# Every engine's instructions in one written order of 1785 steps, parameter loads on three queues, and two row tiles in one FFT step

## The chip, the cores and the metric

The kernel runs on one core of one Trainium2 chip. The metric is the device time in microseconds (us) of one execution. The kernel before takes 423.82 us (the median of 3 runs, 423.2 to 435.42). A core has five engines, each with its own stream of instructions that it works through in order: PE (TensorE, matrix products into the eight PSUM banks), DVE (VectorE, elementwise), ACT (ScalarE, functions, and here all copies out of PSUM), POOL (GpSimd) and SP (SyncE). Here POOL and SP mostly issue DMAs. Semaphores make an instruction wait for what it needs from another engine or from a DMA.

## What is computed

Two independent parts with 2048 positions and 640 channels each, put side by side in the output. Cut to what matters:

```python
# A: attention over a dilated window of 8 positions (32 heads of 20)
qkv = (x @ wqkv).reshape(B, S, 3, H, Dh)             # q, k, v per head
idx = pos[:, None] - 2 * jnp.arange(8)[None, :]      # i, i-2, ..., i-14
logits = einsum("bhsd,bhswd->bhsw", q, k[idx]) * Dh ** -0.5   # -1e9 where idx < 0
o = einsum("bhsw,bhswd->bhsd", softmax(logits), v[idx])
a = o.reshape(B, S, D) @ wo

# B: a state-space convolution (192 states per channel)
logdA = dt * (A_re + 1j * A_im)
K = einsum("dn,dnl,dn->dl", C, exp(logdA[:, :, None] * l), dt * (B_re + 1j * B_im)).real   # 2048 taps
y = irfft(rfft(u padded) * rfft(K padded))[:2048] + u * Dskip
```

## The kernel before

**Part A.** Projections (`proj`, L427, letters k, q, v of the order): 15 groups of four matmul chains of 512 columns; ACT copies each out (L428), SP stores it to DRAM (`qd`, `kd`, `vd`). Attention goes by blocks b of 512 positions. `logits` (L): DVE multiplies q with shifted k (tile `prod`, L464), PE sums within heads (L466, `ps_l`), ACT takes the exponential. `norm` (N) divides by the sum. `av` (A, 20 of them): four loads of `vb` from `vd` on SP and POOL (two `vb` buffers), two DVE products `p` (L504, two `p2` buffers), eight matmuls into `ps_o` (L506), a copy to `oT`. `out_proj` (O, 16): ten matmuls (L517, `ps_op`), two copies to `ob` (two buffers), one store on SP (L520).

**Part B.** `partB_prep` loads the six parameter tensors (`nat`, L123), transposes and scales them on PE (`flip`, L142 and L146) and makes `ta` (ACT), `wi` and `Gt` (DVE). The 640 channels then go in five chunks c of 128. `gens` (G) makes the powers of the recurrence: Exp and Sin on ACT, products on DVE, stored to DRAM (`Gdram`) for all chunks but the first. `x_tables` (T loads `Xg`, M computes) and `y_tables` (D decay factors on ACT, W loads, Y computes) build factor tables by complex products on DVE (L226 to L228, L289). `kgen` (K) contracts them on PE: 512 small matmuls a chunk (L303, `ps_k`, one PSUM bank) in three rounds, each copied out by ACT (L305). The kernel K goes through DRAM (l, `kload`) and is spread to 2048 taps (g, `ps_s`). A two-step FFT of u (f) and of K (g): `f1` (L343) and `f2_prod` (x, L363), the product with DVE (L368, `Yf`). Then the inverse: `ia` (y, L378, the matmuls `ps_ia` with the constant `EA`, copied out by ACT to `Z`, L380) and `inverse` (I, L737, `ps_ib`), which needs the 4 MB constant `HB`. `skip` (S) computes u * Dskip from `uq`. `HB` lies in the memory of the tables, which is free when the last K stage has ended. U stages bring u into another layout.

**What sets the order.** `ORDER` lists 144 stages, each a call that emits all its instructions. From these the framework's scheduler makes the order on every engine when the program is built, by readiness and by place in the list; whatever it decides is then fixed, and each engine works through its own list. Part of a stage may so come before another's. PSUM is shared as two banks "a" (`ps_p`, `ps_op`), three "b" (FFT steps), two "l" (attention, transposes), and one for `ps_k`.

Of the kernel before, what the change touches and what calls it, by code (L numbers as in the profile page):

```python
# [17 lines left out]
NCH = 5  # L18
CW = 192
ORDER = "k3 q4 q2 D0 U4 q0 U1 q1 q3 k4 G0 G1 M0 v4 Y0 k1 U7 U0 k0 k2 K0 U5 v0 v1 v2 U6 L0 U3 T1 L1 v3 N0 A0 A1 U2 A2 A3 A4 G3 L2 D1 L3 W1 R0 O2 N1 M1 Y1 T2 O3 O0 l0 f0 M2 K1 D2 O1 g0 x0 W2 T3 Y2 A5 A6 K2 A7 f1 l1 g1 y0 W3 x1 D3 M3 T4 Y3 A8 A9 L4 y1 K3 L5 W4 N2 l2 M4 D4 O6 O5 f2 O4 g2 x2 l3 Y4 O7 A10 y2 K4 S1 S0 f3 A11 g3 A12 A13 A14 O9 O11 x3 y3 O8 L6 O10 S3 L7 f4 l4 N3 A15 S2 g4 A16 A17 A18 x4 A19 I1 I2 y4 S5 I0 S4 S6 I3 I4 S7 O14 O12 I5 O13 I7 I6 O15"  # L20
# [15 lines left out]
XGB = 1  # L36
# [39 lines left out]
def fft_consts_np():  # L76
# [11 lines left out]
    EA = np.zeros((128, 4, 64, 2, 2))  # L88
    for dd in range(2):
        s = slice(64 * dd, 64 * dd + 64)  # L90
        EA[s, 0, :, 0, dd] = np.cos(phi)
        EA[s, 0, :, 1, dd] = np.sin(phi)
        EA[s, 1, :, 0, dd] = -np.sin(phi)
        EA[s, 1, :, 1, dd] = np.cos(phi)
# [8 lines left out]
    return dict(BD1=BD1.reshape(128, 256), T=T.reshape(128, 32 * 2 * 64), EA=EA.reshape(128, 1024), HB=HB.reshape(128, 64 * 2 * 128))  # L103


def partB_prep(tc, pools, prm, Gd):

    nc = tc.nc
    V = nc.vector
    pp, psp, ident, ap = pools["prep"], pools["psum"], pools["ident"], pools["att"]  # L110
    W = NCH * CW
    nat = []
    for tag in ("p2", "p2", "prod"):
        nt = ap.tile([128, 2, NCH, CW], bf16, name="nat", tag=tag, bufs=2)
        nat += [nt[:, 0], nt[:, 1]]
    ldt = pp.tile([128, NCH], bf16, name="ldt")
    lsrc = prm["B_log_dt"].rearrange("(g c t) -> g t c", g=4, c=NCH, t=32)
    for g in range(4):
        nc.scalar.dma_start(out=ldt[32 * g:32 * g + 32, :], in_=lsrc[g])
    for a, nm in enumerate(["B_A_re", "B_A_im", "B_C_re", "B_C_im", "B_B_re", "B_B_im"]):  # L120
        src = prm[nm].rearrange("(g c t) n -> g t c n", g=4, c=NCH, t=32)
        for g in range(4):
            (nc.gpsimd if a in (2, 3) else nc.sync).dma_start(out=nat[a][32 * g:32 * g + 32], in_=src[g])  # L123
    qt = pp.tile([128, 1], f32, name="quarter")
    nc.gpsimd.memset(qt[:], float(np.pi / 2))
    pools["quarter"] = qt
    dtb = pp.tile([128, NCH], bf16, name="dtb")
    nc.scalar.activation(out=dtb[:], in_=ldt[:], func=ACT.Exp)
    dtf = pp.tile([128, NCH], f32, name="dtf")
    V.tensor_copy(out=dtf[:], in_=dtb[:])  # L130
    dg = ap.tile([128, NCH, 128], bf16, name="dg", tag="attn")
    for c in range(NCH):
        V.tensor_scalar(out=dg[:, c, :], in0=ident[:], scalar1=dtf[:, c:c + 1], scalar2=None, op0=A.mult)

    def flip(a, diag, tag="l"):
        psb = [psp.tile([128, 512], f32, name="ps_tr", tag=tag, bufs=2 if tag == "l" else 3) for _ in range(2)]
        for c in range(NCH):
            rhs = dg[:, c, :] if diag else ident[:]
            for h in range(2):
                hs = slice(64 * h, 64 * h + 64)  # L140
                col = c * CW + 64 * h
                nc.tensor.matmul(psb[col // 512][:, col % 512:col % 512 + 64], lhsT=nat[a][:, c, 0:128], rhs=rhs[:, hs], start=True, stop=True, skip_group_check=True)  # L142
            for h in range(2):
                hs = slice(64 * h, 64 * h + 64)
                col = c * CW + 128
                nc.tensor.matmul(psb[col // 512][hs, col % 512:col % 512 + 64], lhsT=nat[a][hs, c, 128:192], rhs=rhs[hs, hs], start=True, stop=True,  # L146
                                 tile_position=(64 * h, 64 * h), skip_group_check=True)
        return [(slice(0, 512), psb[0][:]), (slice(512, W), psb[1][:, 0:W - 512])]

    ta = pools["cst"].tile([128, W], f32, name="ta")  # L150
    wi = pp.tile([128, W], i32, name="wi")
    for s, ps in flip(0, True):
        nc.scalar.copy(out=ta[:, s], in_=ps)
    wk = ap.tile([128, 512], f32, name="wk", tag="qb")
    for s, ps in flip(1, True):
        n = ps.shape[1]
        V.tensor_scalar(out=wk[:, 0:n], in0=ps, scalar1=1.0 / TWO_PI, scalar2=MAGIC, op0=A.mult, op1=A.add)
        V.tensor_scalar(out=wk[:, 0:n], in0=wk[:, 0:n], scalar1=MAGIC, scalar2=None, op0=A.subtract)
        V.scalar_tensor_tensor(out=wk[:, 0:n], in0=ps, scalar=1.0 / TWO_PI, in1=wk[:, 0:n], op0=A.mult, op1=A.subtract)
        V.tensor_scalar(out=wi[:, s], in0=wk[:, 0:n], scalar1=2147483648.0, scalar2=None, op0=A.mult)  # L160
    cc = ap.tile([128, 2, W], bf16, name="cc", tag="prod", bufs=2)
    for i in range(2):
        for s, ps in flip(2 + i, False):
            nc.scalar.copy(out=cc[:, i, s], in_=ps)
    Gt = ap.tile([128, NCH, 2, CW], bf16, name="Gt", tag="oT")
    br, bi = flip(4, True, "b"), flip(5, True)
    pr = [ap.tile([128, W], f32, name="pr", tag=t, bufs=n) for t, n in (("kb", 1), ("vb", 2))]
    for op, c0, c1, r in ((A.subtract, 0, 1, 0), (A.subtract, 1, 0, 1)):
        for (s, b0), (_, b1) in zip(br, bi):
            V.tensor_tensor(out=pr[0][:, s], in0=b0, in1=cc[:, c0, s], op=A.mult)  # L170
            if r == 0:
                V.tensor_tensor(out=pr[1][:, s], in0=b1, in1=cc[:, c1, s], op=A.mult)
            else:
                V.scalar_tensor_tensor(out=pr[1][:, s], in0=b1, scalar=-1.0, in1=cc[:, c1, s], op0=A.mult, op1=A.mult)
        p3 = [pr[q][:].rearrange("p (c n) -> p c n", c=NCH) for q in range(2)]
        if r == 0:
            V.tensor_tensor(out=Gt[:, :, 0], in0=p3[0], in1=p3[1], op=A.subtract)
        else:
            V.tensor_tensor(out=Gt[:, :, 1], in0=p3[1], in1=p3[0], op=A.subtract)
    nc.sync.dma_start(out=Gd[1:, :, NG - 1].rearrange("c p r n -> p c (r n)"), in_=Gt[:, 1:].rearrange("p c r n -> p c (r n)"))  # L180
    return ta, wi, Gt


def gens(tc, pools, ta, wi, ca, cb, dst, done):

    nc = tc.nc
    V = nc.vector
    gp = pools["prep"]
    n = cb - ca
    s = slice(CW * ca, CW * cb)  # L190
    order = [3, 4, 5, 6, 7, 8, 0, 1, 2, 9, 10]
    am = gp.tile([128, 11, 2 * CW], bf16, name="am", tag="am")
    for k in order:
        nc.scalar.activation(out=am[:, k, 0:n * CW], in_=ta[:, s], func=ACT.Exp, scale=float(2 ** k))
    for k in order:
        pht = gp.tile([128, 2 * CW], i32, name="ph", tag="ph", bufs=2)
        mct = gp.tile([128, 2 * CW], f32, name="mc", tag="mc", bufs=2)
        ph, mc = pht[:, 0:n * CW], mct[:, 0:n * CW]
        if dst is None:
            cst = gp.tile([128, 2, 2, CW], bf16, name="cs", tag="cs", bufs=2)  # L200
            cs = cst[:, 0:n]
        else:
            cs = dst(k)
        V.tensor_scalar(out=ph, in0=wi[:, s], scalar1=k + 1, scalar2=None, op0=A.logical_shift_left)
        nc.scalar.activation(out=mc, in_=ph, func=ACT.Abs, scale=PHS)
        v = lambda ap: ap.rearrange("p (c n) -> p c n", c=n)
        nc.scalar.activation(out=cs[:, :, 1], in_=v(ph), func=ACT.Sin, scale=PHS)
        nc.scalar.activation(out=cs[:, :, 0], in_=v(mc), func=ACT.Sin, scale=-1.0, bias=pools["quarter"][:])
        V.tensor_tensor(out=cs, in0=cs, in1=v(am[:, k, 0:n * CW]).unsqueeze(2).to_broadcast([128, n, 2, CW]), op=A.mult)
        done(k, cs)  # L210


def decay(tc, pools, ta, c):


    S = pools["tab"].tile([128, MID, CW], bf16, name="Stab", tag="Stab")
    for k in range(1, MID + 1):
        tc.nc.scalar.activation(out=S[:, k - 1], in_=ta[:, CW * c:CW * c + CW], func=ACT.Exp, scale=float(-16 * k))  # L218
    pools["S", c] = S


def cmul(nc, O, Y, g, t, conj):

    V = nc.vector
    for o, gr in ((O[0], g[0]), (t[0], g[1])):
        V.tensor_tensor(out=o, in0=Y, in1=gr, op=A.mult)  # L226
# [41 lines left out]
def y_tables(tc, pools, Y, c):  # L268
# [12 lines left out]
    for k in range(1, 4):  # L281
        ys(2 ** k + 1, 2 ** k - 1, 2 ** k)
# [527 lines left out]
```

The softmax here doesn't subtract the row's maximum and nothing guards it: scores larger than these inputs give would overflow.

## Time and profile before

| | busy, us | instructions |
|---|---|---|
| PE matmul | 329.0 (78% of 422.1) | 6100 |
| PE weight loads | 211.1 | 6100 |
| DVE | 315.4 (75%) | 472 |
| ACT | 290.4 (69%) | 612 |
| POOL | 85.6 (20%) | 158 |
| DMA | 72.65 MB, mean 172 GB/s | |

The costliest groups are L427 (`ps_p`, 77.1 us for 300 matmuls), L303 (`ps_k`, 51.7 us for 2560), L504 and L464 on DVE (47.8 us each), the copies L346 and L365 on ACT (42.5 and 41.1 us) and L378 (`ps_ia`, 39.5 us for 320 matmuls). An engine's busy time is the union of its records, which can overlap; a line's total can hence count a little more. A wait is put down to what ended it last. "Issue" is time in which an engine waits for nothing that the profile shows. The mean granted clock of PE was 0.903 of full speed.

### The profile page before, as it was taken

The page shows a single profiled execution, that of the slowest core. Times are in us where ns is not written, and L with a number is a line of the kernel's source. Part 1 is how long each engine was busy: PE and PEld are TensorE (multiplying, and loading weights), DVE is VectorE, ACT ScalarE, POOL GpSimd, SP SyncE. Part 2 cuts the span into 40 slices and gives each one's busy share as a digit, 9 for nine tenths or more (in the row PEclk, how much of TensorE's full clock was granted, in tenths as well). Part 3 has the DMA queues.
Part 4 walks back from the last instruction along what each step waited for, and adds up shares of the span by engine and source line. Part 5 has one row for each costly group of instructions (what it writes and reads, how often), then busy time and mean ns, then how long its engine had stood idle before and what let it go on. Part 6 is the DMA issues. An engine that isn't in the chain of part 4 may idle for free.

```text
span 422.1 us, 14233 instructions
## 1 busy us (share of the span) xinstructions
PE 329.0 (78%) x6100; PEld 211.1 (50%) x6100; DVE 315.4 (75%) x472; ACT 290.4 (69%) x612; POOL 85.6 (20%) x158
## 2 busy tenths in 40 slices
PE   0476896989698144897989889958798898978982
PEld 0342342455432013655668657746486756655871
DVE  1339996733998999689999989958997057778472
ACT  1586895999897976267997377734866285789731
POOL 6313350150001233402111201001111022012242
PEclk9999698999999755599999899966998899999996
DMA  7994865686655858627733263242432099646977
GB/s 179 243 213 104 240 178 204 240 247 216 207 136 217 264 155 247 174 75 208 215 107 101 80 202 124 78 129 85 128 114 90 5 313 320 187 167 180 221 145 149
DMA packets 67996, 72.65 MB, mean 172 GB/s; under 512 B 32421, under 2 KB 58261, under 8 KB 67165
## 3 DMA queue, kind: packets, MB, share of 16 engines
q1 hardware_dynamic: 60076, 55.28, 44.8%
q0 software_dynamic: 6496, 15.64, 13.8%
q10 hardware_dynamic: 1360, 0.82, 0.9%
q8 instruction: 48, 0.79, 0.8%
q14 instruction: 16, 0.12, 0.1%
HBM read 44.11 MB, written 24.98 MB: 164 GB/s over the span
## 4 chain that ended last, share of the span: by engine, by line
PE 43%; ACT 21%; DMA 15%; DVE 11%; issue 7%; SPq 1%; DVEq 0%; ACTq 0%
PE ps_k L303 8%; PE ps_ia L378 7%; PE ps_f L343 6%; PE ps_p L427 5%; DMA out_dram<-ob 4%; ACT S L365 4%; PE ps_op L517 4%; PE ps_o L506 3%; ACT A L346 2%; DMA Gdram<-cs 2%; PE ps_l L466 2%; ACT Stab L218 2%; DMA nat<-in_B_A_im_dram 2%; PE ps_f L363 2%; PE ps_ib L737 2%
## 5 line engine op out<-in xcount | busy, mean ns | idle before, releaser
L427 PE MATMUL ps_p<-xT,w 128*128 128x512 bf16 x300 | 77.1, 410 | 13.8 <-ACT st L428 13.3
L303 PE MATMUL ps_k<-Ytab,Xtab 128*20 128x33 bf16 (+1 forms) x2560 | 51.7, 246 | 13.5 <-issue 11.5
L504 DVE TENSOR_TENSOR p<-vb,attn 128x2048 bf16<-128x2048 bf16 x40 | 47.8, 1218 | 17.7 <-PE ps_o L506 16.4
L427 PEld LDWEIGHTS <-w 128*128 128x128 bf16 x300 | 30.1, 103 | 56.5 <-issue 29.8
L303 PEld LDWEIGHTS <-Xtab 128*20 128x20 bf16 (+1 forms) x2560 | 45.0, 126 | 24.0 <-issue 20.6
L464 DVE TENSOR_TENSOR prod<-qb,kb 128x2048 bf16<-128x2048 bf16 x40 | 47.8, 1220 | 7.6 <-PE ps_l L466 5.6
L346 ACT CAST A<-ps_f 128x512 bf16<-128x512 f32 x80 | 42.5, 608 | 10.1 <-PE ps_f L343 10.0
L500 POOL DMA_DIRECT2D vb<-vd x40 | 22.6, 569 | 124.3 <-DVE p L504 118.6
L378 PE MATMUL ps_ia<-cEA,Yf 128*128 128x256 bf16 x320 | 39.5, 279 | 5.5 <-DVE Yf L368 3.5
L365 ACT CAST S<-ps_f 128x512 bf16<-128x512 f32 x80 | 41.1, 621 | 1.6 <-PE ps_f L363 1.3
L517 PE MATMUL ps_op<-wo,oT 128*128 128x320 bf16 x160 | 32.9, 320 | 7.3 <-ACT oT L508 3.6
L428 ACT CAST st<-ps_p 128x512 bf16<-128x512 f32 x60 | 34.0, 581 | 5.3 <-PE ps_p L427 5.3
L380 ACT CAST Z<-ps_ia 128x512 bf16<-128x512 f32 x40 | 23.5, 593 | 20.2 <-PE ps_ia L378 19.5
L378 PEld LDWEIGHTS <-Yf 128*128 128x128 bf16 x320 | 30.7, 100 | 12.9 <-DVE Yf L368 4.7
L363 PE MATMUL ps_f<-A,cT 128*64 128x128 bf16 x640 | 31.5, 222 | 2.7 <-ACT A L346 0.8
L368 DVE TENSOR_TENSOR Yf<-S 128x1024 bf16<-128x1024 bf16 x40 | 25.6, 686 | 6.5 <-ACT S L365 6.5
L506 PE MATMUL ps_o<-p,cG 128*32 128x512 bf16 x160 | 22.2, 437 | 10.6 <-DVE p L504 10.5
L363 PEld LDWEIGHTS <-cT 128*64 128x64 bf16 x640 | 21.8, 109 | 15.5 <-issue 13.8
L305 ACT CAST Kd<-ps_k 128x363 bf16<-128x363 f32 (+1 forms) x15 | 6.7, 450 | 32.1 <-PE ps_k L303 32.1
L226 DVE TENSOR_TENSOR Xtab<-Xtab,Xg 128x1536 bf16<-128x1536 bf16 (+2 forms) x30 | 20.6, 688 | 9.7 <-DMA Xg<-Gdram 9.3
L518 ACT CAST ob<-ps_op 128x320 bf16<-128x320 f32 x32 | 13.1, 429 | 16.8 <-DMA out_dram<-ob 9.3
L343 PE MATMUL ps_f<-cBD,U 128*64 128x128 bf16 x320 | 22.9, 286 | 0.0
(103 smaller groups left out, 575.9 us busy)
## 6 DMA issues: line engine op xcount, KB each, us to landing
vb<-vd SPq DMA_DIRECT2D x40, 128.5 KB
vb<-vd POOLq DMA_DIRECT2D x40, 128.5 KB, 3.7
Gdram<-cs SPq DMA_DIRECT2D x22, 192.0 KB
HB<-k_HB SPq DMA_DIRECT2D x2, 2048.0 KB
Zdram<-Z SPq DMA_DIRECT2D x3, 1024.0 KB
zq<-Zdram SPq DMA_DIRECT2D x12, 256.0 KB
kb<-kd SPq DMA_DIRECT2D x4, 657.5 KB
us<-in_B_u_dram POOLq DMA_DIRECT2D x32, 80.0 KB, 3.4
```

Source lines behind the costliest of these rows:

```text
L303: MM(ps[32 * g:32 * g + 20, i, :], lhsT=X[rows, part % 2, :, col + t0 + i], rhs=Y[rows, :, part % 2, col + t0 + i], start=(part == 0 and i ...
L343: nc.tensor.matmul(ps[64 * r:64 * r + 64, jj], lhsT=src(2 * (4 * jq + jj) + dd), rhs=C["BD1"][:, r, :], start=(jj == 0), stop=True, skip_g ...
L346: nc.scalar.copy(out=A1[:, :, sig, o:o + 16].rearrange("p k (j g) -> p k j g", g=4), in_=ps[:].rearrange("p j (k g) -> p k j g", g=4))
L363: nc.tensor.matmul(ps[64 * dd:64 * dd + 64, kk, r], lhsT=T[:, k, r, :], rhs=A1[:, k, :, 64 * dd:64 * dd + 64], start=(kk == 0 and r == 0), ...
L365: nc.scalar.copy(out=S[:, :, :, :, 2 * h:2 * h + 2, :].rearrange("p r s j k g -> p (r s) j k g"), in_=ps[:].rearrange("p k r s (j g) -> p ...
L378: nc.tensor.matmul(ps[:, jj].rearrange("p l r d -> p (l r d)"), lhsT=Yf[:, q, 2 * jq + jj, :], rhs=C["EA"][:, q, :], start=(jj == 0 and q ...
L427: nc.tensor.matmul(ps[:], lhsT=w[:, kt, 128 * ct:128 * ct + 128], rhs=self.xT[:, kt, 512 * sc:512 * sc + 512], start=(kt == 0), stop=(kt = ...
L428: nc.scalar.copy(out=st[:, sc], in_=ps[:])
L464: V.tensor_tensor(out=pr[:], in0=q[:, ct].unsqueeze(1).to_broadcast([128, 4, PB]), in1=windows(k[:, ct, 2 * u2:2 * u2 + PB], 4, 4), op=A.mult)
L504: V.tensor_tensor(out=p2[:], in0=v[:, :, 2 * u2:2 * u2 + PB], in1=self.at[b][:, u2].unsqueeze(1).to_broadcast([128, 4, PB]), op=A.mult)
L506: nc.tensor.matmul(ps[32 * d:32 * d + 32], lhsT=self.pools["G4"][:], rhs=p2[:, d], start=(u2 == 0), stop=(u2 == 1), tile_position=(0, 32 * ...
L517: nc.tensor.matmul(ps[:], lhsT=self.oT[b][:, t, 128 * x:128 * x + 128], rhs=self.wo_sb[:, t, 320 * eh:320 * eh + 320], start=(t == 0), sto ...
```

## The change

1. **Order.** Each stage is cut into short steps (`st(...)`): one elementwise or ACT instruction, one group of matmuls for one PSUM bank, or one or a few DMA issues; 1785 in all. Tiles are allocated at first use (`Lazy`). Inside `manual_schedule` the program runs the steps in the order of a list of their numbers, and this is the order on all five engines. It is meant to take the order out of the scheduler's hand and to allow the mixing of stages within an engine. The numbers used here: 694 to 708 are K4 (with 697, 702 and 707 the last matmul part of a round), 1554 to 1587 the value stages A10 to A14, 1695 and 1696 the two loads of `HB`, 1598 the store of O9.
2. **First loads.** A_re stays on SP, A_im goes to ACT's queue, the other four parameter tensors to POOL's; of the attention weights q and k go out on ACT, v on POOL.
3. **Two row tiles.** The step `ia` multiplied by a constant that was block-diagonal over the two halves of the partitions. Now each half is a row tile of 64x128 of the array, with 128 columns instead of 256, its own PSUM bank, and `EA` half as large. To that end a half holds channels 0 to 15 or 16 to 31 of a group instead of the even or odd ones.
4. **PSUM.** Three banks "l" (now with projections) and four "b"; `ps_k` keeps its own.

The diff, cut to its core:

```diff
-ORDER = "k3 q4 q2 D0 U4 q0 U1 q1 q3 k4 G0 G1 M0 v4 Y0 k1 U7 U0 k0 k2 K0 U5 v0 v1 v2 U6 L0 U3 T1 L1 v3 N0 A0 A1 U2 A2 A3 A4 G3 L2 D1 L3 W1 R0 O2 N1 M1 Y1 T2 O3 O0 l0 f0 M2 K1 D2 O1 g0 x0 W2 T3 Y2 A5 A6 K2 A7 f1 l1 g1 y0 W3 x1 D3 M3 T4 Y3 A8 A9 L4 y1 K3 L5 W4 N2 l2 M4 D4 O6 O5 f2 O4 g2 x2 l3 Y4 O7 A10 y2 K4 S1 S0 f3 A11 g3 A12 A13 A14 O9 O11 x3 y3 O8 L6 O10 S3 L7 f4 l4 N3 A15 S2 g4 A16 A17 A18 x4 A19 I1 I2 y4 S5 I0 S4 S6 I3 I4 S7 O14 O12 I5 O13 I7 I6 O15"
+ORDER = """
+0 1 2 6 3 9 4 5 14 13 26 7 12 48 47 27 50 28 49 8 29 30 31 32 11 329 330 331 16 332 25 15 326 33 328 34 325 24 35 327 322 43 324 36 323 45 37 10 321
...
+1204 690 1201 1194 1205 1196 1553 1190 1195 1202 1191 1258 691 1203 1555 1197 1583 1208 1220 1640 1209 1563 694 1221 1576 1222 692 1564 1223 1218 1206
+1219 1565 1210 1226 1207 1228 1211 1216 693 1554 1566 1217 1212 1567 1213 1572 695 1570 696 697 1622 1582 1571 698 1624 1573 699 1574 1556 700 1558
+701 1557 1225 702 1639 1586 1559 703 1560 704 1584 705 1224 1575 1585 1214 706 1215 1587 707 1588 1227 1694 1695 708 1739 1242 1229 1697 1243 709 1240
...
+1755 1774 1670 1772 1672 1673 1775 1776 1681 1778 1686 1754 1682 1782 1679 1687 1756 1684 1680 1683 1779 1685 1757 1688 1780 1758 1783 1784 1759 1760
+1691 1674 1692 1689 1675 1676 1690 1693 1677 1678
+"""
...
-    EA = np.zeros((128, 4, 64, 2, 2))
+    EA = np.zeros((128, 4, 64, 2))
...
+class Steps:
+
+
+    def __init__(self):
+        self.names, self.steps = [], []
+
+    def stage(self, name):
+        self.name = name
+
+    def __call__(self, fn):
+        self.names.append(self.name)
+        self.steps.append(fn)
+
+
...
+def run(nc, tc, st):
+    E = mybir.EngineType
+    with tc.manual_schedule(engines={E.PE, E.Activation, E.DVE, E.Pool, E.SP}):
+        for i in ORDER.split():
+            st.steps[int(i)]()
...
-            (nc.gpsimd if a in (2, 3) else nc.sync).dma_start(out=nat[a][32 * g:32 * g + 32], in_=src[g])
+    def ld_nat(a):
+        src = (B_A_re, B_A_im, B_C_re, B_C_im, B_B_re, B_B_im)[a].rearrange("(g c t) n -> g t c n", g=4, c=NCH, t=32)
+        nt, h = nat[a]
+        for g in range(4):
+            (SP, ACTE, PQ)[min(a, 2)].dma_start(out=nt()[32 * g:32 * g + 32, h], in_=src[g])
+
+    for a in range(6):
+        st(lambda a=a: ld_nat(a))
...
+    def bank(shp, name, tag):
+        return Lazy(lambda: psp.tile(shp, f32, name=name, tag=tag, bufs={"l": 3, "b": 4}[tag]))
...
+            for part in range(4):
+                st(lambda part=part, go=go: go(part))
+            st(lambda t0=t0, nt=nt, ps=ps: ACTE.copy(out=Kd[c]()[:, :, t0:t0 + nt], in_=ps().rearrange("p t b -> p b t")))
...
-    for jq in range(8):
-        ps = pools["psum"].tile([128, 2, 64, 2, 2], f32, name="ps_ia", tag="b", bufs=3)
-        for jj in range(2):
-            for q in range(4):
-                nc.tensor.matmul(ps[:, jj].rearrange("p l r d -> p (l r d)"), lhsT=Yf[:, q, 2 * jq + jj, :], rhs=C["EA"][:, q, :],
-                                 start=(jj == 0 and q == 0), stop=(q == 3), skip_group_check=True)
-        nc.scalar.copy(out=Z[:, :, :, 4 * jq:4 * jq + 4].rearrange("p l r (j d) -> p (l r) j d", d=2), in_=ps[:].rearrange("p j l r d -> p (l r) j d"))
...
+        for jq in range(4):
+            ps = [bank([128, 4, 64, 2], "ps_ia", "b") for _ in range(2)]
+
+            def go(jq=jq, ps=ps):
+                for jj in range(4):
+                    for q in range(4):
+                        for dd in range(2):
+                            d = slice(64 * dd, 64 * dd + 64)
+                            MM(ps[dd]()[:, jj].rearrange("p l r -> p (l r)"), lhsT=Yf[c]()[d, q, 4 * jq + jj, :], rhs=EA()[d, q, :],
+                               start=(jj == 0 and q == 0), stop=(q == 3), tile_position=(64 * dd, 0), skip_group_check=True)
+
+            st(go)
+            for dd in range(2):
+                o = 16 * dd + 4 * jq
+                st(lambda o=o, ps=ps, dd=dd: ACTE.copy(out=zc()[:, :, :, o:o + 4].rearrange("p l r j -> p (l r) j"), in_=ps[dd]()[:].rearrange("p j l r -> p (l r) j")))
```

## The prediction

> **What bounds the kernel now.** I read the page's busy times first, then busy time by stretch, then the waits, then the chain of work. The page:
>
> ```profile
> PE 329.0 (78%) x6100; PEld 211.1 (50%) x6100; DVE 315.4 (75%) x472; ACT 290.4 (69%) x612; POOL 85.6 (20%) x158
> ```
>
> No engine is full; three are nearly equal. The change moves instructions more than it removes them, so the question is how much of the 422 us is time in which none of the three works at its limit. By stretch (columns: length, then busy time of PE, weight loads, DVE, ACT, POOL, then granted PE clock, DMA share, GB/s):
>
> ```profile
> 0.00:160.00 160.00, 109.16 (x1056) 50.88 (x1057) 113.61 (x207) 124.31 (x259) 42.62 (x82) 0.90 0.72 204
> 160.00:320.00 160.00, 136.56 (x3282) 98.64 (x3285) 145.22 (x202) 104.81 (x228) 23.66 (x45) 0.89 0.45 135
> 320.00:422.10 102.10, 83.25 (x1777) 61.53 (x1765) 56.61 (x65) 61.25 (x126) 19.34 (x32) 0.93 0.66 180
> ```
>
> The middle is DVE-bound (145 of 160 us). The beginning has no engine over 124 of 160, the end none over 83 of 102: the loss is at the two ends. Cutting the run into 20 us slices and adding up the busiest of PE, DVE and ACT in each gives 362 us, so 422 - 362 = 60 us belong to no engine. Of these, 14 lie before 20 us (ACT busiest, 5.9 of 20) and 9 after 400 us (PE 12.9 of 22.1), which leaves 37 between. The waits show two kinds of loss (total us, times, longest):
>
> ```profile
> DVE p L504 <- PE ps_o L506: 16.4, 3, 14.3
> PE ps_tr L142 <- DMA nat<-in_B_A_im_dram: 14.0, 1, 14.0
> ACT ob L518 <- DMA out_dram<-ob: 9.3, 2, 7.8
> DVE Xtab L226 <- DMA Xg<-Gdram: 9.3, 1, 9.3
> ```
>
> The first is one hole in DVE, 324.4 to 338.8 us: the value products p wait for two p2 buffers that the matmuls ps_o free, and these stand in PE's queue behind the kernel table's matmuls ps_k (L303), which fill PE there. The third is in the chain (start, length, what):
>
> ```profile
> 337.01 0.95 PE ps_k L303 x44
> ...
> 345.07 14.36 DMA out_dram<-ob
> ```
>
> The last ps_k frees the table pool, the 4 MB of HB start at 338 us, and the output rows that hold the two ob buffers need 14.4 us to land behind them. While DVE or ACT stand, PE is busy: such holes cost balance, not the 37. The 37 hold waits for nothing visible ("issue"): those of 0.7 us and more in the chain sum to some 18 us, most of them among the ps_k, where PE takes a matmul and a weight load every 20 ns (51.7 us for 2560).
>
> **What the Trainium skill says.** "TensorE: Matmul & The Clock Gate", Architectural detail: ACT and DVE are strict FIFOs; one late operand stops all behind it, as in the 14.3 us hole. Same page, What's actually happening: an idle PE is throttled to half clock. The trace agrees: 0.55 and 0.51 granted at 140 to 180 us, where PE was busy 6.8 and 14.1 of 20. "DMA: Bandwidth & Descriptors", Issuing engines are not separate DMA queues: more issuing engines save issue time only, since all use the same 16 DMA engines. The DMA share of 0.91 in the first 20 us agrees. "TensorEngine Tiling (Array Packing)", Theoretical Speedup and Gotcha 1: up to 2x from two row tiles, which must write different PSUM banks; the new code gives each its own. No 64x128 tile is in this trace.
>
> **The parts.**
>
> *First loads.* Now SP issues A_re, A_im, B_re, B_im at about 0.9 us an issue, A_im from 4.7 to 8.4 us, while two weight loads of 800 KB go out at 1.3 and 2.6 us; the first matmul starts at 14.0. After, A_im goes out on ACT's queue behind four small issues (1.87 us by now's row), C_im first on POOL, and the two weights only behind A_im. With the DMA engines full either way, the gain is order: 1.6 MB at the 207 GB/s of this stretch (8 us) no longer compete with 1.4 MB of parameters, but the first transpose of x does. ACT spends 6.4 us issuing (1.87 + 4 x 0.9 + 2 x 0.46), within the 8.2 us for which it waits for log_dt anyway. I take the first matmul at 10 us; bounds 8 and 14.
>
> *Two row tiles in the inverse step (L378).* Now 320 matmuls of 256 columns; an undisturbed block:
>
> ```profile
> 306.34 7.22 PE L378 MATMUL ps_ia<-cEA,Yf 128*128 128x256 bf16 x64 [1.46 <-DVE Yf L368]
> ```
>
> That is 113 ns each. After, 640 of 128 columns in 320 pairs. Full overlap: 56 ns a pair, 18 us in all. None: 36 us. The nearest two-tile row, f2 at L363 (two column tiles, 128 columns), has 31.5 us for 640; weights are no floor, since ps_ib does load and matmul of 96 columns in 6.7/128 = 52 ns. I take 25 us against 39.5: PE falls from 329 to 314.5. ACT's 40 copies (Z) of 0.59 us remain, 4.7 us a chunk beside PE's 5, so ACT takes over the pace of this step and no more than the 14.5 can be won; PE's share below uses 314.5. The constant EA halves to 128 KB and the channels of f1 change place: nothing, they lie beside other loads and keep their instruction counts.
>
> *PSUM.* Two banks for ps_p/ps_op, three b and two l become three l and four b. PE waits for ACT st 13.3 us before ps_p now, partly hidden; projections then share with attention. Nothing on balance, up to 5 us either way.
>
> *Steps and order.* The DVE and ACT steps are the same instructions; the Exp/Sin alternations in the list need 19 table loads, against 21 now at 1.28 us. So DVE stays 315 and ACT some 288. I gave each of the 1785 steps the mean of its row in this trace (several instructions times their mean), scaled each engine to its page total (PE to 314.5), since the records of one engine overlap, and cut the list into groups of 119. PE/DVE/ACT in us:
>
> 16/11/18, 16/23/21, 20/25/28, 24/15/25, 20/24/20, 12/27/16, 19/24/18, 24/22/19, 23/18/16, 22/21/19, 22/24/20, 20/25/13, 30/24/16, 21/14/18, 25/20/17.
>
> The busiest engine of each group sums to 364 us, practically the 362 of now: the order balances the engines no better over 25 us. The K4 parts (12, at 1403 to 1462) stand singly between the ps_o of A10 to A14, which closes the DVE hole, and HB is issued at 1466, behind those value loads and 50 steps (10 us) ahead of the next output row. But as much imbalance is elsewhere: the Xg hole stays, with DVE at 15 beside ACT's 25 in the fourth group. So the gain can come only out of the 60 us that belong to no engine.
>
> Start: 10 instead of 14. Tail: 4 instead of 9, since the list ends in four output projections without the 7.8 us wait on ob, and 4.6 us pass now from the last matmul's end to the end of the run. Middle: 37 now. Of the 18 of "issue" I keep 6, because ps_k comes in parts of 44 matmuls (0.9 us) between longer ones[...]; of the other 19 also 6, because within a group the list alternates the engines step by step. That is a judgement; the bounds are 0 and 37. Sum: 364 + 10 + 12 + 4 = 390 us.
>
> The new waits are those of in-order queues: a value load on SP stands before HB and uq, and all of these before the stores; a load that waits for a buffer (two vb) holds all of them, and DVE waits for them one by one.
>
> **Rivals.**
>
> *Waits return elsewhere.* The middle keeps its 37 in other places: 364 + 10 + 37 + 4 = 415. For it: the "issue" idle before weight loads (29.8 us at L427, 20.6 at L303, partly hidden) has no releaser that an order could move. Against it: single parts of 0.9 us can hold up nobody for 14 us.
>
> *Tight fit.* No wait is left in the middle, the row tiles overlap fully (18 instead of 25 us, half of it where PE is the busiest, -3) and the first matmul starts at 8: 364 + 8 + 4 - 3 = 373. For it: 1785 steps leave hardly a block to stand behind. Against it: the DMA engines are 0.91 busy at the start, and no strict queue fits landing times that vary.
>
> *Slower.* The order assumes landing times that the chip doesn't keep. Value loads on POOL land in 3.7 us at the median, in up to 10.9 between 310 and 345 us. If each of the 20 value blocks shows half its landing, 1.85 us, in DVE's queue, that is 37 us on top of 415: 452. For it: DMA share 0.97 at 340 to 360 us. Against it: DVE waits only 1.2 us for vb now with the same two buffers.
>
> **How the numbers follow.** Main course 0.50 (390), waits return 0.22 (415), tight 0.15 (373), slower 0.13 (452). 2% is 8.5 us, so faster is below 415.3, slower above 432.3. Main and tight are faster, of the 415 half, and half of it within 2%: 0.76, 0.11, 0.13. The range runs from 365, the bare sum with start and tail hidden, which is the tight case with its own spread, to 424, the 415 with a spread of 2%; it leaves out the slower case and a little at each end.
>
> **What would show it.** Right: first matmul near 10 us; no DVE idle of 14 us behind ps_o; no 14 us landing of ob in the chain; ps_ia near 25 us busy in 640 matmuls; DVE still near 315 busy and over 80% of the span. Wrong: ps_ia at 35 or more (no overlap of row tiles); DVE or ACT holes on vb, K2, Xg or uq loads that sum to over 40 us; a granted clock below 0.85, which would say that PE starves. If the slices of 20 us, summed as above, give well under 364, the balance was better than my groups say, and the term of the sum is wrong rather than the waits.

## The result, and the profile after

Beside the kernel before on the same chip (426.47 us, the median of 4 runs) the changed kernel takes 407.77 us (404.23 to 408.02): a ratio of 0.957 [0.946, 0.968]. One of the four runs before, at 435.42 us, ran in a slow state and is left out of the ratio. The forecast of 390 against 423.82 was a ratio of 0.920. So the kernel became faster, and the time lies in the range, but half of the expected gain is missing.

Two lines of the page after, the busy time of PE's row and the group of the new row tiles:

```profile
PE 300.9 (74%) x6407; PEld 198.6 (49%) x6420; DVE 312.5 (77%) x472; ACT 284.0 (70%) x610; POOL 90.1 (22%) x165
L689 PE MATMUL ps_ia<-cEA,Yf 64*128 64x128 bf16 x640 | 21.5, 221 | 1.3 <-ACT A L618 0.8
```

The span is 406.0 us. DVE has kept its work (312.5 against 315.4) and takes 77% of the span, short of the 80% that the prediction named. PE has lost 28 us, 18 of them in the row tiles (39.5 to 21.5). So the engines have less to do than I reckoned with, and yet stand longer. The stretches say where. The first 60 us before (length, busy time of PE, weight loads, DVE, ACT, POOL, granted PE clock, DMA share, GB/s):

```profile
0.00:20.00 20.00, 4.95 (x48) 3.12 (x48) 4.32 (x12) 5.92 (x18) 10.64 (x23) 1.00 0.91 207
20.00:40.00 20.00, 14.30 (x94) 7.33 (x93) 12.97 (x34) 15.45 (x48) 4.44 (x9) 1.00 0.82 165
40.00:60.00 20.00, 15.96 (x60) 6.35 (x60) 19.39 (x41) 17.97 (x38) 7.96 (x14) 0.83 0.68 203
```

and after:

```profile
0.00:20.00 20.00, 4.95 (x46) 3.19 (x46) 1.56 (x7) 6.29 (x17) 8.88 (x19) 1.00 1.06 122
20.00:40.00 20.00, 10.03 (x65) 4.86 (x65) 6.91 (x15) 9.22 (x27) 6.15 (x13) 1.00 1.15 157
40.00:60.00 20.00, 13.40 (x56) 5.70 (x58) 14.02 (x37) 11.73 (x35) 7.82 (x12) 0.97 1.07 189
```

The read is the two middle columns and the last two. DVE does 22.5 us of work in 60 us where it did 36.7, ACT 27.2 where it did 39.3. At the same time the DMA engines are busier (a share over 1 means that packet records of one engine overlap) and move less: 122 GB/s in the first slice instead of 207. The transposes of x, issued by SP, are what has moved there. The lines of the instructions on SP that issue them (start, length over all four), before:

```profile
17.57 13.58 SPq L406 DMA_TRANSPOSE xT<-in_A_x_dram  x4
```

and after:

```profile
4.71 41.42 SPq L302 DMA_TRANSPOSE xT<-in_A_x_dram  x4
```

Before, SP issued four parameter tensors ahead of them; now only A_re. So they start 13 us earlier, beside the parameter loads, and SP spends three times as long on them. The waits after (us in all, times, longest) show who pays, and, below the mark, what became of the late holes:

```profile
POOL nat L296 <- DMA nat<-in_B_C_re_dram: 10.1, 4, 8.6
PE ps_tr L359 <- DMA nat<-in_B_A_im_dram: 8.0, 1, 8.0
DVE wk L378 <- PE ps_tr L359: 10.6, 1, 10.6
PE ps_p L555 <- DMA xT<-in_A_x_dram: 8.8, 1, 8.8
...
DVE p L776 <- PE ps_o L781: 4.8, 4, 1.9
DVE krtmp L189 <- DMA Xg<-Gdram: 6.1, 1, 6.1
DVE p L776 <- DMA vb<-vd: 2.7, 2, 1.7
PE ps_s L649 <- DMA K<-Kdram: 3.5, 1, 3.5
ACT ob L798 <- DMA out_dram<-ob: 1.4, 1, 1.4
```

PE starts at 5.4 us with C_im and at 9.4 us with A_re, but stands for A_im until 19.5 us, later than before (16.0), and DVE with it; POOL, by the trace, issues the last part of B_im only when C_re has landed, and stands 8.6 us for it in one piece. The two holes that the prediction wanted closed are closed: `p` behind `ps_o` went from 14.3 us at the longest to 1.9, `ob` behind its stores from 9.3 us in all to 1.4. The chain (start, length, what) confirms both, with one substitute:

```profile
277.21 1.89 PE ps_ia L689 x64
...
341.89 15.06 DMA zq<-Zdram
...
373.45 3.53 DMA out_dram<-ob
```

The 14.4 us in which `ob` landed behind `HB` are now 15.1 us in which `zq` lands behind `HB`.

### The profile page after: what moved, and what is told of

It is laid out like the page before. It is cut to its first block, busy times and chain, and to the rows that moved or that the text cites. A ratio compares the mean times of both kernels' runs of the same rounds, so it can differ in the third digit from the quotient of the medians.

```text
span 406.0 us, 14847 instructions
## 1 busy us (share of the span) xinstructions
PE 300.9 (74%) x6407; PEld 198.6 (49%) x6420; DVE 312.5 (77%) x472; ACT 284.0 (70%) x610; POOL 90.1 (22%) x165
## 3 DMA queue, kind: packets, MB, share of 16 engines
q10 hardware_dynamic: 2720, 1.89, 2.1%
## 5 line engine op out<-in xcount | busy, mean ns | idle before, releaser
L555 PE MATMUL ps_p<-xT,w 128*128 128x512 bf16 x287 | 75.6, 408 | 30.3 <-ACT st L558 16.9
L555 PEld LDWEIGHTS <-w 128*128 128x128 bf16 x300 | 29.6, 103 | 70.4 <-issue 28.3
L529 PE MATMUL ps_k<-Ytab,Xtab 128*20 128x33 bf16 (+1 forms) x2560 | 52.7, 246 | 12.6 <-issue 5.9
L529 PEld LDWEIGHTS <-Xtab 128*20 128x20 bf16 (+1 forms) x2560 | 44.9, 127 | 25.9 <-issue 22.2
L668 PE MATMUL ps_f<-A,cT 128*64 128x128 bf16 x640 | 28.3, 222 | 6.2 <-ACT A L618 2.5
L725 PE MATMUL ps_l<-prod,cGs 128*32 128x512 bf16 x160 | 17.7, 454 | 15.9 <-DVE prod L720 15.7
L795 PE MATMUL ps_op<-wo,oT 128*128 128x320 bf16 x160 | 28.2, 325 | 0.1
L668 PEld LDWEIGHTS <-cT 128*64 128x64 bf16 x640 | 20.7, 109 | 14.6 <-issue 13.6
L571 POOL DMA_DIRECT2D us<-in_B_u_dram x32 | 20.0, 632 | 24.6 <-DMA nat<-in_B_B_im_dram 11.7
L189 DVE TENSOR_TENSOR krtmp<-Xtab,Xg 128x1536 bf16<-128x1536 bf16 (+2 forms) x30 | 20.5, 685 | 6.3 <-DMA Xg<-Gdram 6.1
L490 ACT ACTIVATE Stab<-ta 128x192 bf16<-128x192 f32 x80 | 23.7, 362 | 0.3 <-DVE Ytab L512 0.2
L695 ACT CAST Z<-ps_ia 128x512 bf16<-128x512 f32 x40 | 21.4, 599 | 3.5 <-PE ps_ia L689 3.3
L689 PE MATMUL ps_ia<-cEA,Yf 64*128 64x128 bf16 x640 | 21.5, 221 | 1.3 <-ACT A L618 0.8
L613 PEld LDWEIGHTS <-U 128*64 128x64 bf16 x320 | 20.2, 205 | 3.7 <-issue 2.5
```

Of the source, the lines that this page charges most:

```text
L529: MM(ps()[32 * g:32 * g + 20, i, :], lhsT=X[c]()[rows, part % 2, :, col + t0 + i], rhs=Y[c]()[rows, :, part % 2, col + t0 + i], start=(par ...
L555: MM(ps()[:], lhsT=w()[:, kt, 128 * ct:128 * ct + 128], rhs=xT()[:, kt, 512 * sc:512 * sc + 512], start=(kt == 0), stop=(kt == 4))
L613: MM(ps()[64 * r:64 * r + 64, jj], lhsT=src(16 * dd + 4 * jq + jj), rhs=BD1()[:, r, :], start=(jj == 0), stop=True, skip_group_check=True, ...
L668: MM(ps()[64 * dd:64 * dd + 64, kk, r], lhsT=T()[:, k, r, :], rhs=A1[c]()[:, k, :, 64 * dd:64 * dd + 64], start=(kk == 0 and r == 0), stop ...
L689: MM(ps[dd]()[:, jj].rearrange("p l r -> p (l r)"), lhsT=Yf[c]()[d, q, 4 * jq + jj, :], rhs=EA()[d, q, :], start=(jj == 0 and q == 0), sto ...
L795: MM(ps()[:], lhsT=oT[b]()[:, t, 128 * x:128 * x + 128], rhs=wo_sb()[:, t, 320 * eh:320 * eh + 320], start=(t == 0), stop=(t == 4))
```

## The experiments

All ratios are to the kernel before on the same chip, with 95% intervals. The theory that the traces above suggest: the written order and the row tiles gain about what was expected, and the new loads take back part of it, because transposes that run beside the parameter loads slow them down and the lost start isn't won back. The rival: the loads cost nothing, and the order simply gains less.

| kernel | loads | row tiles | banks | order | ratio to before |
|---|---|---|---|---|---|
| before | old | no | old | scheduler | 1 |
| e8_before_psum | old | no | new | scheduler | 0.989 [0.983, 0.996] |
| e4_before_row_tiles | old | yes | old | scheduler | 1.018 [1.011, 1.025] |
| e2_before_new_loads | new | no | old | scheduler | 1.059 [1.049, 1.069] |
| e10_scheduler | old | yes | new | scheduler, steps | 1.015 [1.011, 1.018] |
| e7_order_only | old | no | new | written | 0.943 [0.937, 0.950] |
| e3_no_row_tiles | new | no | new | written | 0.974 [0.966, 0.982] |
| e1_loads_back | old | yes | new | written | 0.924 [0.916, 0.932] |
| after | new | yes | new | written | 0.957 [0.946, 0.968] |
| e9_transposes_held | new, held | yes | new | written | 0.920 [0.911, 0.929] |

### The loads, each way round

e1_loads_back is the changed kernel with the loading queues and their order of before:

```diff
-            (SP, ACTE, PQ)[min(a, 2)].dma_start(out=nt()[32 * g:32 * g + 32, h], in_=src[g])
+            (PQ if a in (2, 3) else SP).dma_start(out=nt()[32 * g:32 * g + 32, h], in_=src[g])
...
-        st(lambda i=i: (PQ if i == 2 else ACTE).dma_start(out=wqkv[i]()[:], in_=wsrc[:, :, D * i:D * i + D]))
+        st(lambda i=i: (ACTE if i == 1 else PQ).dma_start(out=wqkv[i]()[:], in_=wsrc[:, :, D * i:D * i + D]))
```

> The changed kernel with the first loads put back to the queues and the order of before (A and B parameters on SP, C on POOL, weight q first on POOL, k on ACT, and the transposes of x behind the four parameter tensors on SP); the rest of the written order is kept. Theory 1 (the early transposes of x starve the parameter loads, and what DVE loses in the first 60 us is not won back): the four transposes are issued within 15 us instead of 41, DVE has some 35 of the first 60 us busy instead of 22.5, and the time falls by 10 to 15 us, to 393 to 398. Theory 2 (the stretch from 60 to 160 us is bound by ACT and takes up a late start): the start is earlier but the time stays within 4 us of the changed kernel.

Measured: 398.31 us, 0.924 [0.916, 0.932]. Its first 60 us, in one stretch:

```profile
0.00:60.00 60.00, 37.14 (x202) 17.56 (x206) 32.38 (x72) 37.33 (x99) 25.89 (x47) 0.89 0.84 193
```

DVE is at 32.4 us of work instead of 22.5, the DMA share below 1. The new loads cost 3.3% of the time before, some 14 us.

e2_before_new_loads puts only the new queues into the kernel before:

```diff
-            (nc.gpsimd if a in (2, 3) else nc.sync).dma_start(out=nat[a][32 * g:32 * g + 32], in_=src[g])
+            (nc.sync, nc.scalar, nc.gpsimd)[min(a, 2)].dma_start(out=nat[a][32 * g:32 * g + 32], in_=src[g])
...
-            (nc.scalar if i == 1 else nc.gpsimd).dma_start(out=t[:], in_=src[:, :, D * i:D * i + D])
+            (nc.gpsimd if i == 2 else nc.scalar).dma_start(out=t[:], in_=src[:, :, D * i:D * i + D])
```

> The kernel before with the new queues of the first loads only (A_im on ACT, B on POOL, weights q and k on ACT), so that the transposes stand on SP right behind A_re. Theory 1: the transposes take some 40 us to issue here too and the time rises by 10 to 15 us, to 435 to 442. Theory 2: within 4 us of before.

Measured: 1.059 [1.049, 1.069], some 25 us, in the direction of the theory and larger than it said. Its stretch and its longest waits:

```profile
0.00:60.00 60.00, 18.80 (x134) 10.02 (x137) 10.58 (x27) 16.87 (x48) 16.48 (x33) 1.00 0.97 128
```

```profile
ACT cc L164 <- PE ps_tr L142: 33.2, 1, 33.2
DVE pr L170 <- PE ps_tr L142: 25.3, 1, 25.3
PE ps_p L427 <- DMA xT<-in_A_x_dram: 17.0, 1, 17.0
```

Read from below: here the scheduler put projections, which need x transposed, ahead of later parameter transposes on PE. PE stands 17 us for x, the `ps_tr` behind it come at 43.6 us, and ACT and DVE wait for those. The same delay of the DMAs costs more where a strict order puts the starved load ahead of work that is ready.

e9_transposes_held keeps the three queues, but a copy of 16 KB that reads B_im stands ahead of the transposes on SP, so that they start when the last parameters are there. The order of the loads on each of the three queues stays:

```diff
-0 1 2 6 3 9 4 5 14 13 26 7 12 48 47 27 50 28 49 8 29 30 31 32 11 329 330 331 16 332 25 15 326 33 328 34 325 24 35 327 322 43 324 36 323 45 37 10 321
+0 1 2 6 3 4 5 14 13 26 7 8 1785 9 12 48 47 27 50 28 49 29 30 31 32 11 329 330 331 16 332 25 15 326 33 328 34 325 24 35 327 322 43 324 36 323 45 37 10 321
...
+    hold = dpool.tile([128, 64], bf16, name="hold")
+    st(lambda: SP.dma_start(out=hold[:], in_=nat[5][0]()[:, nat[5][1], 0, 0:64]))
```

> The kernel after with its three loading queues kept, but SyncE waits for the last parameter load (a small copy that reads B_im stands ahead of the four transposes), so that the transposes start behind the parameter loads. If the early transposes are what delays the parameter loads, 393 to 400 us (ratio near 0.925, that of the version with the loads of before), with parameter loads landing near 7 to 8 us and transposes that take some 14 us. If it is the spread over three queues itself, the ratio stays near 0.957 and the parameter loads land as late as in the changed kernel.

Measured: 394.29 us, 0.920 [0.911, 0.929]. SP starts the transposes at 19.1 us and spends 15.7 on them. What the DMAs do in these two kernels (size of one, median us from issue to landing), first after:

```profile
w<-in_A_wqkv_dram POOLq DMA_DIRECT2D x1, 800.0 KB, 18.1
nat<-in_B_B_re_dram POOLq DMA_DIRECT2D x4, 60.0 KB, 15.6
```

then with the transposes held:

```profile
w<-in_A_wqkv_dram POOLq DMA_DIRECT2D x1, 800.0 KB, 8.0
nat<-in_B_B_re_dram POOLq DMA_DIRECT2D x4, 60.0 KB, 8.5
```

Half the landing time, same queues. And the first 60 us:

```profile
0.00:60.00 60.00, 36.14 (x216) 17.89 (x220) 34.54 (x74) 39.71 (x105) 31.74 (x57) 0.97 0.89 207
```

DVE and ACT are back at 34.5 and 39.7, and POOL, with the same issues in the same order, at 31.7 instead of 22.9. So it is the early transposes and not the three queues. Nor is the lost start won back: DVE runs the same 472 instructions in the same order in both kernels, and in the trace of after the thirty-sixth starts 12.6 us later than with the transposes held (at 53 us), the last one 14.4 us later. "DMA: Bandwidth & Descriptors" of the Trainium skill, Issuing engines are not separate DMA queues, says that more issuing engines save issue time only; held transposes with three queues (0.920) and the old queues (0.924) agree with that within their intervals.

### Row tiles and banks

e3_no_row_tiles puts the old full-array `ps_ia` into the changed kernel, with its order and banks kept; e7_order_only does the same with the loads of before. The edit, the same in both:

```diff
-                for jj in range(4):
-                    for q in range(4):
-                        for dd in range(2):
-                            d = slice(64 * dd, 64 * dd + 64)
-                            MM(ps[dd]()[:, jj].rearrange("p l r -> p (l r)"), lhsT=Yf[c]()[d, q, 4 * jq + jj, :], rhs=EA()[d, q, :],
-                               start=(jj == 0 and q == 0), stop=(q == 3), tile_position=(64 * dd, 0), skip_group_check=True)
+                for hf in range(2):
+                    for jj in range(2):
+                        for q in range(4):
+                            MM(ps[hf]()[:, jj].rearrange("p l r d -> p (l r d)"), lhsT=Yf[c]()[:, q, 4 * jq + 2 * hf + jj, :], rhs=EA()[:, q, :],
+                               start=(jj == 0 and q == 0), stop=(q == 3), skip_group_check=True)
```

> The changed kernel with the inverse FFT step again as 320 matmuls of 256 columns over all 128 rows (block-diagonal constant), in the same places of the order. If the step is on the path that sets the end: PE busy rises by 17 us (39 for the step instead of 21.5) and the time by 5 to 10 us, to 413 to 418. If its copies on ACT or DVE work set the pace: PE busy rises as much and the time by less than 3 us.

> The written order and the banks alone: the loads of before and no row tiles. If the three parts add up (loads +14, row tiles -7, and the rest the order and the banks): 0.94 of the kernel before. If the order owes its gain to the row tiles (PE shorter than DVE only with them): over 0.97.

Measured: 0.974 and 0.943. Row tiles are worth 1.7% (0.974 to 0.957) with the new loads and 1.9% (0.943 to 0.924) with the old; the new loads cost 3.1% without row tiles and 3.3% with them. Within the intervals, the effects add up. The profiles are less even. In e3_no_row_tiles DVE does 27.6 us of work in the first 60, where after did 22.5 with the same loads, and from 40 us up to its 306th instruction, at 233 us, it is only 3 to 5 us behind e7_order_only; at the last one it is 12.8 us behind. So the start doesn't cost the same in every execution, and where the later 8 us of this one come from is not shown.

e8_before_psum gives the kernel before the new banks alone:

```diff
-        ps = self.psp.tile([128, PB], f32, name="ps_o", tag="l", bufs=2)
+        ps = self.psp.tile([128, PB], f32, name="ps_o", tag="l", bufs=3)
...
-            ps = self.psp.tile([128, 512], f32, name="ps_p", tag="a", bufs=2)
+            ps = self.psp.tile([128, 512], f32, name="ps_p", tag="l", bufs=3)
```

> The kernel before with the banks of after (three shared by projections, attention and output projections, four for the FFT steps) and the scheduler's order. If the banks are part of the gain: 5 us less or more. If PE's 13 us of waits before ps_p grow, since projections now share with attention: slower. Prediction of the first study: within 5 us either way.

Measured: 0.989 [0.983, 0.996]. So from this version to e7_order_only, which has the same banks, loads and matmuls, the written order is worth 0.046, some 20 us.

e4_before_row_tiles gives the kernel before the row tiles alone (`ia`, `EA` and the channel order of `f1`, three banks "b" as they were):

```diff
-    for jq in range(8):
-        ps = pools["psum"].tile([128, 2, 64, 2, 2], f32, name="ps_ia", tag="b", bufs=3)
+    for jq in range(4):
+        ps = [pools["psum"].tile([128, 4, 64, 2], f32, name="ps_ia", tag="b", bufs=3) for _ in range(2)]
```

> The kernel before with the row tiles alone. The 640 matmuls take 20 to 23 us of PE busy instead of 39.5 (they overlap in pairs, 30 to 35 ns each in an undisturbed block). If the step's 7% of the chain was worth something: 416 to 421. If the scheduler's order leaves PE to wait for ACT's copies instead: within 3 us of before.

Measured: 1.018 [1.011, 1.025], slower, which no theory expected. PE is at 332.2 us and hasn't fallen, and the row tiles take 34.2 us, not the 20 to 23 that were expected:

```profile
L380 PE MATMUL ps_ia<-cEA,Yf 64*128 64x128 bf16 x640 | 34.2, 235 | 5.5 <-ACT Z L384 3.0
```

One matmul has a median of 216 ns in the records here and after, but that doesn't show the overlap: within a block their starts lie 42 ns apart on the mean at the full granted clock (29 after), and 135 of the 640 run at half of it (32 after). So about a third of the row tiles' own gain is left in this order. The order also costs time elsewhere: the scheduler has changed it on every engine, and DVE is 4.6 us behind already between 60 and 160 us, long before the first `ps_ia` at 226 us. What displaced the matmuls, and how the slowdown divides between these, is not shown.

### The order

e10_scheduler takes the steps, banks and row tiles of e1_loads_back, emits them stage by stage in the old stage list, and leaves the order to the scheduler:

```diff
-    with tc.manual_schedule(engines={E.PE, E.Activation, E.DVE, E.Pool, E.SP}):
-        for i in ORDER.split():
-            st.steps[int(i)]()
+    for s in STAGES.split():
+        order += [i for i, n in enumerate(st.names) if n == s]
+    for i in order:
+        st.steps[i]()
```

> The steps of the changed kernel with its row tiles and PSUM banks and the loads of before, but ordered by the framework's scheduler in place of the written order. If the written order carries the gain, a ratio near 0.97 (banks 0.989 by row tiles 0.98), and near 1.0 if the scheduler spoils the row tiles as it did when they were put into the kernel before alone. If cutting the kernel into steps and the banks are enough, near 0.924 as with the written order.

Measured: 434.56 us, 1.015 [1.011, 1.018]. The 0.090 to e1_loads_back, some 39 us, is the order alone. It is twice the 0.046 found without row tiles, since the scheduler loses again with row tiles and the written order gains; the row tiles take 26.5 us here and 21.9 in e1_loads_back. Cutting into steps by itself brings nothing here. The wait that the prediction started from tells the scheduler's versions from the written ones. e8_before_psum:

```profile
DVE p L504 <- PE ps_o L506: 16.4, 2, 15.5
```

e10_scheduler:

```profile
DVE p L780 <- PE ps_o L785: 15.0, 1, 15.0
```

e7_order_only, with the written order:

```profile
DVE p L775 <- PE ps_o L780: 7.9, 5, 3.4
```

The same balance for all, in 20 us slices (the busiest of PE, DVE and ACT summed, and what is left of the profiled span):

| | busiest engine | none | span |
|---|---|---|---|
| before | 362 | 60 | 422 |
| e8_before_psum (scheduler) | 361 | 63 | 424 |
| e7_order_only (written) | 355 | 47 | 402 |
| e10_scheduler (row tiles, scheduler) | 360 | 71 | 431 |
| e1_loads_back (row tiles, written) | 347 | 51 | 398 |
| after | 343 | 63 | 406 |
| e9_transposes_held | 347 | 44 | 392 |
| e12_tables_in_blocks | 364 | 76 | 440 |

From the scheduler's order to the written one (e8 to e7, e10 to e1), 15 and 20 us of time that belongs to no engine go, and 6 and 12 us in better balance.

e12_tables_in_blocks starts from e9_transposes_held and puts the twelve matmul parts of each kernel table, with their copies, together again:

```diff
+        for c in range(NCH):
+            blk = [i for i in order if st.names[i] == f"K{c}"][:-1]
+            at = order.index(blk[-1])
+            order = [i for i in order[:at] if i not in blk] + blk + order[at + 1:]
```

> The version with the transposes held, but the 12 matmul parts of each of the five kernel tables (ps_k), with the ACT copies of their bank, stand together where the last copy stood, so that PE has five blocks of some 10 us again; nothing else moves. If the single parts between DVE's and ACT's work are what the written order gains by, each block opens a hole of up to 10 us in DVE or ACT, and the ratio to the kernel before rises from 0.920 to between 0.945 and 0.97 (10 to 20 us), with DVE waits behind ps_o or ps_l of 5 us and more. If the placing of these parts matters little and the order gains elsewhere, it stays within 1% of 0.920.

Measured: 443.79 us, 1.043 [1.035, 1.050], 0.12 or some 52 us above e9_transposes_held: the direction of the first theory, at more than twice its size. Its waits:

```profile
ACT Kd L539 <- PE ps_k L534: 55.0, 15, 6.2
DVE prod L725 <- PE ps_l L730: 14.1, 4, 11.7
DVE Yf L680 <- ACT S L677: 24.9, 4, 12.8
```

and, of e9_transposes_held:

```profile
ACT Kd L534 <- PE ps_k L529: 11.4, 6, 5.0
DVE prod L720 <- PE ps_l L725: 3.0, 4, 1.0
DVE Yf L675 <- ACT S L672: 4.2, 4, 1.4
```

and a stretch of e12_tables_in_blocks around one block:

```profile
240.00:260.00 20.00, 15.07 (x588) 11.75 (x582) 8.59 (x12) 6.98 (x15) 2.19 (x5) 0.76 0.23 66
```

The expected hole is there in each of the five blocks, and all five count: DVE stands for 8.3, 11.7, 11.4, 12.5 and 12.8 us, 57 in all, where I had let 10 to 20 count. Three of these holes end with ACT, one with PE and one with a load of `Ytab`. Each copy stands in ACT's queue straight behind the parts that it copies, so ACT waits through nearly the whole block, 55 us in 15 copies, and DVE runs dry behind it (8.6 of 20 us above). "TensorE: Matmul & The Clock Gate" of the Trainium skill, Architectural detail, calls ACT and DVE strict FIFOs, so what stands behind a waiting copy waits with it; here the trace prices it at 3.7 us a copy. The mean granted clock is 0.831 too, against 0.899 with the transposes held; whether that is a cost of its own or follows from the holes is not separated. The edit is blunt: it moves the copies too, and what a block costs with the copies set further back was not tried.

### The late wait on zq

e5_hb_after_zq puts the two loads of `HB` behind those of `zq` and `uq` in the changed kernel, e6_loads_hb does so in e1_loads_back, e11_held_hb in e9_transposes_held:

```diff
-701 1557 1225 702 1639 1586 1559 703 1560 704 1584 705 1224 1575 1585 1214 706 1215 1587 707 1588 1227 1694 1695 708 1739 1242 1229 1697 1243 709 1240
-1696 1230 1241 1236 1699 1232 1231 1577 1259 1233 1741 1261 1237 1235 1578 1238 1579 1265 1260 1262 1263 1234 1266 1623 1580 1264 1626 1625 1267 1581
+701 1557 1225 702 1639 1586 1559 703 1560 704 1584 705 1224 1575 1585 1214 706 1215 1587 707 1588 1227 1694 708 1739 1242 1229 1697 1243 709 1240
+1230 1241 1236 1699 1232 1741 1695 1231 1577 1259 1233 1696 1261 1237 1235 1578 1238 1579 1265 1260 1262 1263 1234 1266 1623 1580 1264 1626 1625 1267 1581
```

> The changed kernel with the two 2 MB loads of HB moved behind the first two loads of zq and of uq on SP (eight DMAs go ahead of them), the rest of the order kept. In the changed kernel the chain waits 15 us for zq to land behind HB. If that wait sets the time from there on: 5 to 10 us less, 398 to 403. If HB itself is needed as early (the matmuls ps_ib take HB too), or if the stretch has other work: within 3 us of the changed kernel.

> Both repairs, the loads of before and HB behind zq and uq. If the two costs are independent: the sum of their gains, 385 to 393. If the late part has slack: the same as the loads alone.

> The same with the HB loads behind the zq loads. As HB behind zq gave nothing beside the loads of before (0.921 against 0.924), within 1% of the version with the transposes held alone; a gain of 3 us or more would say that the late waits on zq cost time once the start is short.

Measured: 0.943 [0.934, 0.952], 0.921 [0.912, 0.929] and 0.922 [0.912, 0.933]. In e5_hb_after_zq the 15 us of `zq` leave the chain. It looks like a gain of 1.4%, within the intervals of the two kernels, but the start also happened to be better (28.0 us of DVE work in the first 60 us for 22.5): DVE is 6.4 us ahead of the changed kernel at its thirty-sixth instruction and 3.7 us at its last, so nothing was won late. Beside a good start nothing is won either (0.921 for 0.924, 0.922 for 0.920). These two say less about `zq`, which stands in the chain of neither e1_loads_back nor e9_transposes_held; in e6_loads_hb it is `HB` that stands there, landing for 17.4 us. The waits of the changed kernel already held the answer:

```profile
PE ps_ib L851 <- DMA zq<-Zdram: 0.4, 1, 0.4
```

A long link in the chain was worth nothing, since PE had other work beside it and stood for `zq` 0.4 us in all.

## Why the prediction was right, and where it wasn't

The kernel became faster and its time lies in the range, but 18 us above the forecast, and the main argument, that the gain can come only out of time that belongs to no engine, fails for the changed kernel. The sum, 364 + 26 (10, 12 and 4), measures 343 + 63 by the same slices, where the kernel before had 362 + 60: all of the gain is in the first term, and what the order won among the waits the start has eaten. That the time still lies in the range is partly luck: one term was 21 us too high, the other 37 too low. With the transposes held it is 347 + 44, and both terms gain, some 15 and 16. Point by point:

- *First loads* (first matmul at 10 us, start 10 instead of 14): this step failed, and costs the missing time. The first matmul does come early, at 5.4 us, below the bound of 8, since C_im is first on POOL and its transposes need neither A nor log_dt. But the slices lose 13.7 us before 20 us, where 10 stood, and another 10.0 from 20 to 40 and 6.0 from 40 to 60, 30 us in all (the kernel before loses 14.1, 4.6 and 0.6 there, 19). The prediction saw that the first transpose of x would compete with the parameters, set it against the two weight loads, and didn't ask what transposes do to the loads beside them. With the transposes held (e9_transposes_held), A_im's matmuls do start at 10.7 us, and the three slices lose 17.
- *Row tiles* (25 us, 18 to 36): 21.5 us, nearly full overlap. The chain's 64 matmuls in 1.89 us are 59 ns a pair against 113 ns for a full-array matmul of 256 columns. That is 1.9x of the "up to 2x" in "TensorEngine Tiling (Array Packing)" of the Trainium skill, Theoretical Speedup. "No more than 14.5 won" held with room: 7 to 8 us with the written order. Under the scheduler the overlap was not a given (34.2 us in e4_before_row_tiles).
- *Balance* (364, "the order balances the engines no better"): this term was mis-sized, and the prediction's last sentence on what would show it applies: the sum over the slices is well under 364. With the old loads the order sums to 355 without row tiles and to 347 with them, so 17 of the 21 us are balance and PE work that I didn't see; the other 4 probably come with the poor start, whose work lies in later slices beside other work. I gave each step the mean of its row before, as if busy time were fixed. But PE's total falls from 329.0 to 312.0 in e7_order_only with the same matmuls (`ps_op` from 32.9 to 26.5, `ps_o` from 22.2 to 16.4, at means of 320 to 311 and 437 to 420 ns): their records overlap more. Half of that is not the order's: with the banks alone (e8_before_psum) PE is at 320.9 us already, and `ps_op` at 26.9. The groups of the prediction were also a little off: as printed, PE's sum to 318 us and not to 314.5.
- *Middle* (12 instead of 37, between 20 and 400 us): mis-sized too. From 60 to 400 us, past the three slices of the start, the kernel before loses 32 us and the changed one 28; from 60 to 380 the kernel before loses 31 and the one with the transposes held 22. So 4 to 9 went, not 25. The idle of "issue", of which I had kept 6 of 18, did not go with shorter parts: ahead of the weight loads of `ps_p` and `ps_k` it was 29.8 and 20.6 us before and is 28.3 and 22.2 now, partly hidden in both.
- *K4 parts close the DVE hole; HB behind the value loads*: right, 14.3 to 1.9 us and no long wait on `vb`. e12_tables_in_blocks shows what single parts are worth when their copies stand close behind. *Xg hole stays*: right, 6.1 us after 9.3.
- *Tail* (4): right, 5.4 us after 400 us.
- *PSUM* (nothing, up to 5 either way): 1.1% by itself, 5 us.

The rivals: *slower* by landing times falls, since DVE waits for `vb` 2.7 us in all and not 37. *Tight fit* (373) needed all of the middle to go, and even with the transposes held 44 us belong to no engine. *Waits return elsewhere* (415) comes nearest in number, and in part it is what happened: waits returned, but most of them at the start, which that rival left at 10. That 390 is close to the 394 us of e9_transposes_held is two errors that cancel: 17 us less for the busiest engine and 18 more for none.

Open remains why the scheduler loses time with row tiles (1.018 and 1.015, against 0.989 with the banks alone). The step itself overlaps worse or runs at half clock there, but it is still shorter than without row tiles; the mean granted clock is lower too (0.855 and 0.869, against 0.884), as cause or as consequence. The orders differ everywhere, and no run separates one displaced stage. Open also is why the early transposes are slow themselves: no run has them beside the parameter loads or the weight loads alone.

## What to carry to other kernels

Spreading loads over more queues changes what is first in each queue: ask for every queue what now starts earlier, and whether the loads that the first instructions wait for can stand it. Here one small load ahead of the transposes on the same queue, which waits for the last parameters, brought the changed kernel from 0.957 to 0.920, the best version (e1_loads_back, e6_loads_hb and e11_held_hb are equal to it within their intervals). In a written order, short matmul parts set singly between the other engines' steps are worth more than the balance of totals shows, and a copy that stands in its queue long before its bank is full holds up what stands behind it (here for 3.7 us each).

## What the runs showed of the hardware

DMA transposes beside ordinary loads: SP spent 2.9 to 3.9 us on each of four (13.6 in all) in the kernel before, and 3.4 to 16.2 us on each (41.4 in all) when they started at 4.7 us. Loads of 60 KB issued by POOL beside them landed in 15.6 us; with the transposes held it was 8.5.

A high DMA share isn't a high rate: in the first 20 us the DMA engines showed a share of 1.06 at 122 GB/s after, and 0.91 at 207 GB/s before, with transposes only in the last 2.4 us. The transposes alone don't make the low rate: from 18 to 31 us in the kernel before, with the transposes issued behind the parameter loads, the share was 1.14 at 211 GB/s.

Two row tiles: 64 matmuls of 64x128 took 1.89 us where they overlapped. The same 640 took 21.5 us in all after, 26.5 in e10_scheduler and 34.2 in e4_before_row_tiles, at a median of 216 ns for one in each: the length of one record doesn't tell whether tiles overlap.
